# Leaving out two fills with zeros between the attention stage and the experts of a fused kernel

## The chip, the cores and the metric

One core of a Trainium2 chip runs one program. The metric is the device time of an execution in microseconds (us); less is better. The engines named below are TensorE (PE, with its weight loads as PEld), VectorE (DVE), ScalarE (ACT), GpSimd (POOL) and SyncE (SP), which issues most transfers.

## The reference, cut to what matters

```python
for t in range(S):                                   # attention: 2 x 8 heads, 768 steps, 48 wide
    state = alpha[:, :, t, :, None] * state + einsum('bhd,bhe->bhde', k[:, :, t], v[:, :, t])
    y[:, :, t] = einsum('bhd,bhde->bhe', q[:, :, t], state)
# x = y as 1536 tokens of 384 values
expert_idx = argmax(x @ w_gate, axis=1)              # one of 8 experts for each token, softmax weight gate_w
for i in range(N):                                   # at most `capacity` tokens for one expert
    if counts[e] < capacity: disp[e, counts[e]] = x[i]; pos[i] = counts[e]; counts[e] += 1
y = relu(disp[e] @ w1[e]) @ w2[e]                    # 384 -> 1024 -> 384
out[i] = gate_w[i] * y[expert_idx[i], pos[i]]
h = out @ w_in                                       # second block, 384 -> 2048 -> 384
return (h * clip(h + 3, 0, 6) / 6) @ w_out
```

## The kernel before, in words

The program has three stages, and the order of the work in each is written out by hand, engine by engine; every engine takes its instructions in that order, and an instruction that waits holds up those behind it on its engine.

**Attention and routing** (to about 122 us). The tokens are 12 tiles of 128. The work goes through 48 pairs (head pair, chunk of 128 tokens). After each tile its logits are turned into an expert and a place, and GpSimd scatters the tile's rows, multiplied by their gates, to a table `xdisp` in memory that has 256 rows for each of the 8 experts (`scatter`, line 119). For the first ten tiles this is done here. Tiles 10 and 11 are ready last, and for the first expert they take another way: `near` (lines 494 to 517) finds out on VectorE which of the tile's tokens go to expert 0 and builds from it a matrix `P` of 128 x 256 that has each token's gate at its place; `near_mm` (line 522) multiplies the tile with it; `near_rows` (line 530) adds the rows of the ten tiles before, which `read_x(0)` (line 226, on SP's queue) has read back from `xdisp` into `xr`. The steps of `near` for the last tile, tile 11, are these; `lgn` are its logits, `m` is their maximum, `g` is a result of TensorE in PSUM:

```python
501  nc.vector.tensor_reduce(out=lg, in_=x[:, t, :, 48:56]..., axis=AX.X, op=ALU.add)
502  nc.vector.tensor_reduce(out=m, in_=lg, axis=AX.X, op=ALU.max)
504  nc.vector.tensor_scalar(out=ls, in0=lg, scalar1=m, scalar2=None, op0=ALU.subtract)
505  nc.vector.tensor_tensor(out=o0[:, n:n + 1], in0=lg[:, 0:1], in1=m, op=ALU.is_ge)
507  nc.scalar.activation(out=ex, in_=ls, func=ACTF.Exp, accum_out=s)
512  nc.tensor.matmul(out=g[:, 0:1], lhsT=upto, rhs=o0[:, n:n + 1], start=False, stop=True)
513  nc.vector.tensor_scalar(out=s, in0=s, scalar1=1e-9, scalar2=None, op0=ALU.add)
514  nc.vector.reciprocal(out=rec, in_=s)
516  nc.vector.tensor_scalar(out=P, in0=place, scalar1=g[:, 0:1], scalar2=rec, ...)
```

The end of the stage on TensorE is, in this order: `near_mm` of tile 10 (line 522, six matmuls), the three small matmuls of tile 11 that give `g` (lines 509, 511, 512), `near_rows` (line 530, twelve matmuls), `near_mm` of tile 11 (line 522, six matmuls). As each third of the sum is ready, `split_x` makes of it the two parts `xhi` (line 236, ScalarE) and `xlo` (line 237, VectorE) that the experts' matmuls read.

**Experts** (to about 287 us). For each expert eight hidden tiles of 128: `l1` (line 761, nine matmuls for each tile, then `hh` on ScalarE and `hl` on VectorE, lines 766 and 767) and `l2` (line 782, nine matmuls). Weights come on SP's queue through three buffers (line 251) and are split in two parts on ScalarE (`whi`, line 262) and on VectorE or GpSimd (`wlo`, line 274). In between, `finish` (lines 184 to 219) sends the last two tiles to the other experts: GpSimd issues two scatters of `xc` (line 119), then the read of expert 1's rows (line 226), then twelve scatters of token numbers and their read (line 219). From expert 1 on the rows come from `xdisp` and are transposed on TensorE (line 747).

The outputs of an expert go to two arrays in SBUF, `xth` and `xtl`, of 128 partitions x 3 x 1792 values (1536 tokens and one slot of 256). Each expert writes 256 columns from its own offset on, which is read from `offi` at run time (lines 786 and 787), and what lies behind its tokens is written over by the next expert. At the start of the stage, ahead of the first `l1`, stand the fills that the change is about:

```python
799  for t in (xth, xtl):
800      nc.gpsimd.memset(t.bitcast(F32), 0.0)
```

The two arrays lie in memory that tiles of the attention stage used before.

**Second block** (to the end). 2 groups of 768 tokens by 16 hidden tiles: `m1` (line 863) reads columns 0 to 1535 of `xth` and `xtl`, `m2` (line 891) gives the rows that GpSimd scatters to the output.

Of the kernel before, what the change touches and what calls it, by code (L numbers as in the profile page):

```python
# [7 lines left out]
F32 = mybir.dt.float32  # L8
# [10 lines left out]
NP = 8          # head pairs (batch x 4)  # L19
SEQ = 768  # L20
C = 128         # chunk of tokens
NC = SEQ // C
NT = 12         # token tiles
# [3 lines left out]
FE = 8          # 128-wide hidden tiles of one expert  # L27
F2 = 16         # 128-wide hidden tiles of the second block
SLOT = 256      # rows held for one expert
NEAR_T = 10     # the tiles from here on reach the first expert on a way of their own  # L30
HW = 56         # value columns and gate columns of one head
RP = 112        # rows of a head pair: 48, 16 of padding, 48
HR = ((0, 64), (64, RP))    # rows of the two heads
GT = 768        # tokens in one group of the second block
PIECES = {0: ((0, 1), (1, 3), (3, 6)), 1: ((0, 2), (2, 6))}  # chunks that become ready together
TAIL = 3        # hidden tiles of the second block that are left to the end
OWN = 4096      # marks a token of the first expert: larger than any place


# Doubles come as pairs of words. A single has the sign, the top bit and the last 7 bits of the double's  # L40
# exponent, and the first 23 bits of its fraction. As a single, a double's upper word orders like the
# double itself: TINY and HUGE are the words of 2**-127 and of the last double below 2**128, times 2**16,
# which turns the second bit of the word's exponent into that of the result.
TINY = 2.0 ** -15 * 2.0 ** 16
HUGE = (1.875 - 2.0 ** -23) * 2.0 ** 16 * 2.0 ** 16


def to_single(nc, out, raw):
    """out[P, N] = the doubles of raw[P, N, 2] as singles, cut to 24 bits; below 2**-126 it gives 0 or less
    than 2**-126."""  # L50
    lo, hi = raw[:, :, 0], raw[:, :, 1]
    bits = out.bitcast(I32)
    nc.scalar.activation(out=out, in_=hi.bitcast(F32), func=ACTF.Abs, scale=65536.0)
    yield
    nc.vector.tensor_scalar(out=out, in0=out, scalar1=TINY, scalar2=HUGE, op0=ALU.max, op1=ALU.min)
    yield
    nc.vector.tensor_scalar(out=bits, in0=bits, scalar1=4, scalar2=1, op0=ALU.logical_shift_left,
                            op1=ALU.logical_shift_right)
    yield
    nc.vector.scalar_tensor_tensor(out=bits, in0=lo, scalar=29, in1=bits, op0=ALU.logical_shift_right,  # L60
                                   op1=ALU.bitwise_or)
    yield
    nc.vector.scalar_tensor_tensor(out=bits, in0=hi, scalar=-2147483648, in1=bits, op0=ALU.bitwise_and,  # L63
                                   op1=ALU.bitwise_or)
# [3 lines left out]
def tile_kernel(ctx: ExitStack, tc: tile.TileContext, qka, vtok, vT, wg64, wg, cap, consts,  # L68
# [38 lines left out]
    # of the last two tiles: values and logits  # L107
# [9 lines left out]
    def scatter(group, dst, idx, src, rows):  # L117
        # every row goes to a place of its own, so scatters need no order among themselves
        ins = nc.gpsimd.indirect_dma_start(  # L119
            out=dst, out_offset=bass.IndirectOffsetOnAxis(ap=idx, axis=0),  # L120
            in_=src, in_offset=None, bounds_check=rows - 1, oob_is_err=False)
        tc.declare_no_dep(ins.ins, group=group, reason="rows of scatters are disjoint")
        tc.add_to_no_dep_group(group, ins.ins)
        scattered.setdefault(group, []).append(ins.ins)
# [8 lines left out]
    def gating(pl, lg, o, po, cum, g, t0, n, res):  # L133
        """Of n tiles of logits: one-hot o of the expert, place po among its tokens, gate weight gt (0 past
        the capacity). The yields let other work in between."""
# [7 lines left out]
        # the first expert with the largest logit: its entry of idxrev is the largest  # L143
# [29 lines left out]
    def rows(pl, t0, n, res):  # L173
        # row of the dispatch: SLOT * expert + position, out of reach from position SLOT on
        po = pos[:, t0:t0 + n]
        rr = pl.tile([128, n], F32, tag=f"rr{n}", name="rr")
        nc.vector.scalar_tensor_tensor(out=rr, in0=po, scalar=float(SLOT), in1=res["r"][:, :, 0],
                                       op0=ALU.is_lt, op1=ALU.mult)
        di = pl.tile([128, n], I32, tag=f"di{n}", name="di", bufs=4)
        nc.vector.scalar_tensor_tensor(out=di, in0=rr, scalar=float(SLOT * NE), in1=po,  # L180
                                       op0=ALU.subtract, op1=ALU.add, reverse0=True)
        return di

    def finish(ps):
        """The last two tiles to the other experts, and where each expert's tokens go in the second block."""
# [36 lines left out]
    def read_x(e):  # L222
        t = xe_p[e % 2].tile([128, 2, DM], F32, tag="xr", name="xr")
        # SP's queue has weights behind; GpSimd's has the scatters before
        eng = nc.gpsimd if e == 1 else nc.sync
        ins = eng.dma_start(out=t, in_=xdisp[e * SLOT:(e + 1) * SLOT].rearrange("(c p) d -> p c d", p=128))
        if e < 3:
            after_scatters("disp", ins)
        xr[e] = t
# [49 lines left out]
    # ================= attention and routing =================  # L279
    with ExitStack() as actx:  # L280
# [34 lines left out]
        def load_piece(p, n):  # L315
            # a piece's columns of decays, keys and queries, and the first of the next
            c0, c1 = PIECES[p][n]
            lo, hi = c0 * C + (n > 0), min(c1 * C + 1, SEQ)
            for o in (2 * SEQ, 0, SEQ):
                nc.sync.dma_start(out=raw[p][:, o + lo:o + hi], in_=qka[p, :, o + lo:o + hi])  # L320
# [117 lines left out]
        def stage_b(p, c):  # L438
# [18 lines left out]
            # each head's scores meet the values of both; its own half is read  # L457
# [32 lines left out]
        # The first expert starts before the rows of the last two tiles come back from memory: products with  # L490
        # a matrix that holds each token's gate at its place put them among the rows of the tiles before.
# [44 lines left out]
        def warm_up(n):  # L536
            # TensorE runs at half its clock until it has been busy for a while
            g = ps_g.tile([128, 512], F32, tag="g", name="g")
            for _ in range(n):
                nc.tensor.matmul(out=g, lhsT=ones, rhs=warm, start=True, stop=True)  # L540
# [5 lines left out]
        with tc.manual_schedule():  # L546
# [56 lines left out]
            for i, (p, c) in enumerate(iters):  # L603
# [7 lines left out]
                if i == 12:  # L611
                    nc.gpsimd.tensor_scalar(out=upto, in0=ident, scalar1=float(OWN), scalar2=None, op0=ALU.mult)
                    nc.gpsimd.tensor_tensor(out=upto, in0=upto, in1=cst[:, 256:384], op=ALU.add)
                    # OWN + place; OWN - 1 past the capacity
                    nc.gpsimd.tensor_scalar(out=place, in0=iota1, scalar1=capf, scalar2=None, op0=ALU.is_le)
                    nc.gpsimd.tensor_tensor(out=place, in0=place, in1=iota1, op=ALU.mult)
                    nc.gpsimd.tensor_scalar(out=place, in0=place, scalar1=float(OWN - 1), scalar2=None, op0=ALU.add)
# [62 lines left out]
    # ================= experts =================  # L680
# [37 lines left out]
    def advance_f():  # L718
        # one step of the work on the second block's weights
# [11 lines left out]
    with ExitStack() as ectx:  # L731
# [59 lines left out]
        with tc.manual_schedule():  # L791
# [7 lines left out]
            for t in (xth, xtl):  # L799
                nc.gpsimd.memset(t.bitcast(F32), 0.0)  # L800
# [3 lines left out]
            for i in range(n):  # L804
# [21 lines left out]
                # GpSimd takes over where VectorE has more of the second block's weights to do  # L826
# [12 lines left out]
    # ================= second block, tokens in the order of the experts =================  # L839
    with ExitStack() as fctx:  # L840
# [60 lines left out]
        # ---- the steps above hold where no decay exceeds 1, chunks decay by no more than 1e-15 and  # L901
        # no expert has more than SLOT tokens; the flag says that one of these fails
# [7 lines left out]
        def check():  # L910
# [6 lines left out]
            # 1 where all is well  # L917
# [13 lines left out]
        with tc.manual_schedule():  # L931
            seq = [(g, f) for g in range(2) for f in range(F2)]
            m1(*seq[0])
            for i, (g, f) in enumerate(seq):
                if i + 1 < len(seq):
                    m1(*seq[i + 1])
                # the last ones tile by tile, so that the rows go out while others are at work
# [20 lines left out]
def general_path(tc, nc, gating, ident, cst, capf, b3, qka, vT, wg, wpack, fpack, out, before):  # L958
    """The same computation for any decays and any load of the experts, with no thought of speed."""
    vr = vT.rearrange("k p t -> (k p) t")  # L960
    GN = 512
    with ExitStack() as ctx:
# [8 lines left out]
        # attention: the state of each (key, value) column by a scan over all tokens  # L971
        with tc.tile_pool(name="g_a", bufs=1) as a_p, tc.tile_pool(name="g_aps", bufs=1, space=PSUM) as aps:
# [29 lines left out]
            # gating of all tokens at once  # L1002
# [55 lines left out]
        # experts: every token by every expert, weighted by its gate  # L1058
# [10 lines left out]
        # second block  # L1069
# [91 lines left out]
```

## Time and profile before

| what | us |
|---|---|
| three runs | 502.42, 504.25, 505.02 |
| their median | 504.25 |
| span of the profiled execution, first to last instruction | 501.6 |

The page of the profile gives the profiled execution's span and no other time for it; the fastest of the three runs is 0.8 us longer than that span, the median 2.65 us. Busy shares of the span: PE 92%, PEld 87%, DVE 66%, ACT 50%, POOL 36%. The mean granted TensorE clock is 0.948 of full speed. All times in the rows below are counted from the span's start; "idle before" in square brackets is how long the engine stood idle before an instruction and what ended that.

### The profile page before, as it was taken

Reading aid. Unit: us, or ns where it says so; the run is one execution under the profiler, and the core shown is the slowest. Engines: PE = TensorE matmul, PEld = TensorE weight load, DVE = VectorE, ACT = ScalarE, POOL = GpSimd, SP = SyncE. Lnnn points to the kernel's source line nnn. Section 1 sums busy time; section 2 is a strip of 40 time slices with the busy share of each in tenths; the row PEclk is TensorE's granted clock in tenths of the full one; section 3 lists DMA queues with packets and bytes.
Section 4 is the critical chain, followed back from the end, with each engine's and each line's share of the span. In section 5 each row is a group of like instructions: output and inputs, shape, how many; then the busy total and the mean of one; then the engine's idle time right before and its main releaser. Section 6 shows DMA issues by size and latency. Waiting matters only on the chain.

```text
span 501.6 us, 8487 instructions
## 1 busy us (share of the span) xinstructions
PE 460.5 (92%) x3148; PEld 438.6 (87%) x3148; DVE 332.7 (66%) x647; ACT 251.4 (50%) x573; POOL 181.6 (36%) x133
## 2 busy tenths in 40 slices
PE   7959969997796899999999999999899999999993
PEld 4758858887695899899999999888899999999993
DVE  6768998577673688888877669888833444444341
ACT  3536645775143677677677554544433433333341
POOL 3335965864457054555545501221200220000003
PEclk8987985899598999999999999999999999999998
DMA  7999892141057697677776102332100031100002
GB/s 194 273 231 294 228 327 65 47 144 64 0 139 148 170 303 246 199 251 265 268 255 219 65 29 98 125 117 75 54 1 0 34 118 57 55 1 0 3 1 101
DMA packets 27539, 66.03 MB, mean 132 GB/s; under 512 B 2896, under 2 KB 14448, under 8 KB 26816
## 3 DMA queue, kind: packets, MB, share of 16 engines
q1 hardware_dynamic: 25408, 60.26, 40.1%
q0 software_dynamic: 2080, 5.13, 2.9%
q8 instruction: 27, 0.44, 0.4%
q14 instruction: 24, 0.20, 0.1%
HBM read 57.51 MB, written 7.87 MB: 130 GB/s over the span
## 4 chain that ended last, share of the span: by engine, by line
PE 48%; issue 22%; DVE 16%; DMA 4%; ACT 4%; POOL 2%; SPq 1%; another core or an unknown queue 0%; POOLq 0%; ACTq 0%; DVEq 0%
PE o L782 13%; PE h L761 13%; PE h L863 5%; PE y L464 4%; PE o L891 4%; DVE gl L877 4%; PE s L423 3%; DMA qka<-in_qka_dram 3%; PE y L461 2%; DVE fc L60 2%; ACT gh L874 2%; POOL out_dram L119 2%; DVE A L358 2%; DVE fc L63 2%; PE u L447 1%
## 5 line engine op out<-in xcount | busy, mean ns | idle before, releaser
L877 DVE SCALAR_TENSOR_TENSOR gl<-t,gh 128x384 fp32r<-128x384 f32 x64 | 47.9, 748 | 36.2 <-ACT gh L874 35.3
L274 POOL TENSOR_TENSOR wlo<-wraw,whi 128x768 fp32r<-128x768 f32 x24 | 51.1, 2135 | 55.9 <-ACT whi L262 41.6
L262 ACT ACTIVATE whi<-wraw 128x768 fp32r<-128x768 f32 (+1 forms) x68 | 55.0, 808 | 25.7 <-PE o L782 24.0
L867 ACT ACTIVATE r<-h,b 128x384 f32<-128x384 f32 x64 | 36.6, 572 | 60.2 <-PE h L863 60.1
L871 DVE SCALAR_TENSOR_TENSOR t<-r,h 128x384 f32<-128x384 f32 x64 | 35.2, 550 | 46.6 <-ACT r L867 46.5
L891 PE MATMUL o<-fh,gl 128*128 128x384 f32 x192 | 64.1, 334 | 0.0
L891 PE MATMUL o<-fh,gh 128*128 128x384 f32 x192 | 64.1, 334 | 0.0
L891 PE MATMUL o<-fl,gh 128*128 128x384 f32 x192 | 64.1, 334 | 0.0
L119 POOL DMA_INDIRECT out_dram<-o,ids x12 | 12.0, 1000 | 124.1 <-DVE o L897 120.5
L782 PE MATMUL o<-hh,whi 128*128 128x256 f32 x192 | 54.5, 284 | 2.3 <-DVE xtl L787 1.4
L274 DVE TENSOR_TENSOR wlo<-wraw,whi 128x768 fp32r<-128x768 f32 (+1 forms) x41 | 42.9, 1047 | 19.7 <-ACT whi L262 17.6
L782 PE MATMUL o<-hl,whi 128*128 128x256 f32 x192 | 54.5, 284 | 1.2 <-DVE hl L767 1.0
L782 PE MATMUL o<-hh,wlo 128*128 128x256 f32 x192 | 53.9, 281 | 0.0
L712 POOL TENSOR_TENSOR fl<-fc,fh 128x768 fp32r<-128x768 f32 x16 | 31.0, 1938 | 63.1 <-ACT fh L710 63.1
L874 ACT ACTIVATE gh<-t 128x384 fp32r<-128x384 f32 x64 | 33.4, 523 | 39.9 <-DVE t L871 39.9
L863 PE MATMUL h<-xth,fh 128*128 128x384 f32 x192 | 45.0, 341 | 4.8 <-DVE t L871 4.7
L863 PE MATMUL h<-xtl,fh 128*128 128x384 f32 x192 | 43.7, 335 | 0.0
L863 PE MATMUL h<-xth,fl 128*128 128x384 f32 x192 | 43.6, 334 | 0.0
L402 ACT ACTIVATE kh<-qka,ra 64x128 f32<-64x128 f32 x96 | 38.1, 397 | 6.8 <-POOL qka L369 3.0
L863 PEld LDWEIGHTS h<-xth,fh 128*128 128x128 f32 x192 | 33.5, 188 | 7.7 <-DVE t L871 7.0
L761 PE MATMUL h<-xhi,whi 128*128 128x256 f32 x192 | 36.6, 296 | 3.8 <-issue 3.7
L782 PEld LDWEIGHTS o<-hh,whi 128*128 128x128 f32 x192 | 36.5, 190 | 3.0 <-DVE xtl L787 1.6
(168 smaller groups left out, 1099.4 us busy)
## 6 DMA issues: line engine op xcount, KB each, us to landing
wraw<-in_wpack_dram SPq DMA_DIRECT2D x32, 768.0 KB, 4.4
fr<-in_fpack_dram SPq DMA_DIRECT2D x16, 768.0 KB, 5.5
qka<-in_qka_dram SPq DMA_DIRECT2D x6, 1011.1 KB, 12.6
xdisp<-warm SPq DMA_DIRECT2D x1, 3072.0 KB
al<-in_qka_dram SPq DMA_DIRECT2D x8, 339.1 KB, 3.0
xr<-xdisp SPq DMA_DIRECT2D x7, 384.0 KB, 4.9
vx<-in_vtok_dram SPq DMA_DIRECT2D x6, 224.0 KB, 5.2
vx<-in_vtok_dram SPq DMA_DIRECT2D x2, 672.0 KB, 19.3
```

The lines of the kernel that those rows point to most:

```text
L262: nc.scalar.activation(out=w_sp[i][0][:, cols], in_=w_raw[i][:, cols], func=ACTF.Copy)
L274: eng.tensor_tensor(out=lo[:, cols], in0=w_raw[i][:, cols], in1=hi.bitcast(F32)[:, cols], op=ALU.subtract)
L402: nc.scalar.activation(out=t[r0:r1, h, :], in_=kb[p][r0:r1, c * C:(c + 1) * C], func=ACTF.Copy, scale=ra[p][r0:r1, c:c + 1])
L712: nc.gpsimd.tensor_tensor(out=lo, in0=t, in1=hi.bitcast(F32), op=ALU.subtract)
L761: nc.tensor.matmul(out=ps[:, 0:SLOT], lhsT=a[:, kk * 128:(kk + 1) * 128], rhs=b[:, kk, :], start=(n == 0), stop=(n == 8))
L782: nc.tensor.matmul(out=yo[e][d][:, 0:SLOT], lhsT=a[:, c0:c0 + 128], rhs=b, start=(f == 0 and n == 0), stop=(f == FE - 1 and n == 2))
L863: nc.tensor.matmul(out=ps[:, 0:384], lhsT=a[:, kk * 128:(kk + 1) * 128], rhs=b[:, kk, c0:c0 + 384], start=(n == 0), stop=(n == 8))
L867: nc.scalar.activation(out=r, in_=ps[:, 0:384], func=ACTF.Relu, bias=b3)
L871: nc.vector.scalar_tensor_tensor(out=t, in0=r, scalar=6.0, in1=ps[:, 0:384], op0=ALU.min, op1=ALU.mult)
L874: nc.scalar.activation(out=gh[:, sl], in_=t, func=ACTF.Copy, scale=1.0 / 6.0)
L877: nc.vector.scalar_tensor_tensor(out=gl[:, sl], in0=t, scalar=1.0 / 6.0, in1=gh.bitcast(F32)[:, sl], op0=ALU.mult, op1=ALU.subtract)
L891: nc.tensor.matmul(out=po[g][t][:, 0:DM], lhsT=a[:, t * 128:(t + 1) * 128], rhs=b[:, 384:768], start=(f == 0 and n == 0), stop=(f == F2 - ...
```

## The change: the fills of `xth` and `xtl` are not issued

```diff
@@ experts, ahead of the first l1
-            for t in (xth, xtl):
-                nc.gpsimd.memset(t.bitcast(F32), 0.0)
             step(3)
             l1(0)
```

Lines behind it move up by two (`values_load`, line 822, becomes line 820). Comments are taken out as well, without moving other lines.

On GpSimd, at the seam between attention and experts, the row of the order that the two programs have there (`xs` and `xc` are rows of tokens, `di` their places, `xdisp` the table in memory, `xr` the rows read back):

```order
 L485 TENSOR_SCALAR xs<-x,gt 128x384
 L119 DMA xdisp<-xs,di 2048x384 x5
-L800 MEMSET xth 128x5376
-L800 MEMSET xtl 128x5376
 L119 DMA xdisp<-xc,di 2048x384 x2
 L226 DMA xr<-xdisp 128x2x384
```

The two fills are gone and nothing else on GpSimd has changed its place; on the other engines the order of the instructions is the same as before. What changes beside that are waits. On GpSimd, the same place in the changed program with the semaphores that each instruction waits for:

```order
L119 DMA xdisp<-xs,di 2048x384 [waits DVE_49,Activation_49] x4
L119 DMA xdisp<-xc,di 2048x384 [waits DMAHW1_49,DVE_49,Activation_49]
L119 DMA xdisp<-xc,di 2048x384 [waits DMASW3_49,DVE_49,Activation_49]
L226 DMA xr<-xdisp 128x2x384 [waits DMASW4_49,DMASW3_49,DMASW5_49,DMASW2_49,DMASW6_49,DMASW1_49,DMASW7_49,DMASW0_49,PE_49]
L119 DMA idsd<-tokid,si 1536x1 [waits DVE_49]
```

The wait for TensorE (`PE_49`) stood at the first fill before; it now stands at the read of expert 1's rows, whose buffer lies in memory of the attention stage too. The first scatter of `xc` waits for ScalarE as well. The first writes of `xth` and `xtl` (lines 786 and 787) waited for GpSimd, and wait for it no longer.

## Rows read from the trace of the kernel before

**Rows 1.** Stretches: us, busy PE, PEld, DVE, ACT, POOL, granted clock, DMA share, GB/s.
```profile
121.50:126.20 4.70, 1.31 (x8) 0.99 (x8) 4.34 (x4) 0.36 (x3) 4.67 (x2) 0.94 0.00 2
...
180.00:230.00 50.00, 48.89 (x412) 48.43 (x411) 41.38 (x63) 35.74 (x68) 27.65 (x13) 1.00 0.75 254
```

**Rows 2.** Chain that ended last, 121 to 137 us: start us, us, what.
```profile
122.22 3.91 DVE ls L504
...
126.96 3.85 DVE P L516
```

**Rows 3.** Timeline of POOL: start us, us, engine, line, operation [idle before].
```profile
121.53 4.58 POOL L800 MEMSET xth<- 128x5376 f32 x1 [4.12 <-PE y L464]
126.05 4.60 POOL L800 MEMSET xtl<- 128x5376 f32 x1
```

**Rows 4.** Timeline of DVE, tile 10's steps, then tile 11's.
```profile
118.86 0.23 DVE L504 TENSOR_SCALAR ls<-lgn,m 128x8 f32<-128x8 f32 x1
119.00 0.15 DVE L505 TENSOR_TENSOR o<-lgn,m 128x1 bf16<-128x1 f32 x1
...
120.09 0.42 DVE L516 TENSOR_SCALAR P<-place,g,rec 128x256 f32<-128x256 f32 x1
...
122.03 0.16 DVE L502 TENSOR_REDUCE m<-lgn 128x1 f32<-128x8 f32 x1
...
126.50 0.15 DVE L513 TENSOR_SCALAR s<-s 128x1 f32<-128x1 f32 x1 [0.37 <-ACT ex L507]
```

**Rows 5.** Timeline of PE, 121 to 136 us.
```profile
121.30 1.04 PE L522 MATMUL s<-P,xc 128*128 128x256 f32 x4
122.18 0.59 PE L522 MATMUL kp<-P,xc 128*128 128x256 f32 x2
...
122.64 0.16 PE L511 MATMUL g<-o,ones 128*128 128x1 bf16 x1
126.21 0.16 PE L512 MATMUL g<-o,upto 128*128 128x1 bf16 x1 [3.41 <-DVE o L505]
126.24 2.06 PE L530 MATMUL s<-cst,xr 128*128 128x128 f32 x8
...
130.85 2.08 PE L522 MATMUL s<-P,xc 128*128 128x256 f32 x4 [1.70 <-DVE P L516]
...
135.90 0.52 PE L761 MATMUL h<-xhi,whi 128*128 128x256 f32 x3
```

**Rows 6.** Busy time by stretch, where the granted clock changes (columns as in rows 1).
```profile
125.50:126.00 0.50, 0.00 (x0) 0.00 (x0) 0.50 (x2) 0.00 (x0) 0.50 (x1) 0.62 0.00 0
...
127.00:131.00 4.00, 2.30 (x12) 2.00 (x10) 3.79 (x1) 0.00 (x0) 3.65 (x1) 0.50 0.00 0
...
135.80:136.20 0.40, 0.40 (x5) 0.40 (x5) 0.00 (x0) 0.00 (x0) 0.00 (x0) 0.92 0.00 0
```

**Rows 7.** Chain of the attention stage: four matmuls of 128 columns at full clock.
```profile
115.96 0.46 PE s L423 x4
```

**Rows 8.** Timelines of ACT and DVE: the last third of expert 0's rows is split.
```profile
133.81 0.39 ACT L236 ACTIVATE xhi<-kp 128x256 fp32r<-128x256 f32 x1 [0.47 <-PE kp L522]
...
134.23 0.42 DVE L237 TENSOR_TENSOR xlo<-kp,xhi 128x256 fp32r<-128x256 f32 x1 [0.43 <-ACT xhi L236]
```

**Rows 9.** SP's queue: the read of expert 0's rows, and its time to landing.
```profile
119.09 0.37 SPq L226 DMA_DIRECT2D xr<-xdisp  x1
...
DMA to landing us min/median/max: 3.0/3.0/3.0
```

**Rows 10.** VectorE's groups by form: the gates of the last two tiles.
```profile
L193 DVE TENSOR_SCALAR xc<-xc,gt 128x384 f32<-128x384 f32 x2 | 0.7, 414 | 0.0
```

**Rows 11.** Timeline of ACT: a later wait, in expert 0.
```profile
156.26 0.39 ACT L236 ACTIVATE xhi<-t 128x256 fp32r<-128x256 f32 x1 [3.27 <-remote]
```

**Rows 12.** Timelines of POOL and PE: expert 1's rows are read, then transposed.
```profile
144.28 0.78 POOL L226 DMA_DIRECT2D xr<-xdisp  x1 [2.31 <-issue]
...
149.52 0.38 PE L747 MATMUL t<-cst,xr 128*128 128x128 f32 x2
```

## The prediction

> **What bounds the kernel now.** I read the stages first. Through the experts TensorE is the bound: in the 50 us of [rows 1]'s second stretch it works 48.89 us at full clock. The stretch at 121.50, where the fills run, is another matter: TensorE works 1.31 us of 4.70, while VectorE and GpSimd look full, and the transfers move 2 GB/s. Then I read the chain of waits there. It does not go through GpSimd at all. It goes through two small VectorE instructions of the last tile, `ls` and `P`, with 3.91 and 3.85 us [rows 2]. The same two lines took 0.23 and 0.42 us one tile earlier [rows 4]. So something holds VectorE, and the timeline of GpSimd says what: the fill of `xth` runs from 121.53 to 126.11, the fill of `xtl` from 126.05 to 130.65 [rows 3]. `ls` starts at 122.22 and ends at 126.13, 0.02 us after the first fill; `P`, whose instruction record is 3.83 us long, ends at 130.79, 0.14 us after the second. Other VectorE instructions ran at their usual speed inside the fills: `m` took 0.16 us, `s` 0.15 us [rows 4]. I read this as two instructions of one kind (a tensor and a scalar per partition) that wait until GpSimd's fill has ended, and not as a VectorE that is slow as a whole.
>
> TensorE pays three times. It waits 3.41 us for `o`, the instruction right behind `ls`, and 1.70 us for `P` [rows 5]. And the granted clock: TensorE is idle from 122.80 on (122.64 + 0.16, [rows 5]), and in the stretch 125.50:126.00 the clock falls to a mean of 0.62; full speed is back only in 135.80:136.20 (0.92) [rows 6]. In between it runs at 1.2 GHz instead of 2.4.
>
> **The change, part by part.** *Removed:* two fills on GpSimd, 4.58 + 4.60 = 9.18 us of that engine [rows 3]. On GpSimd itself they cost nothing now: its next work stands behind the sums of `finish`, which come later than the fills. What counts is what they hold up. I follow the last tile without them.
>
> 1. `ls` starts at 122.22 as now, since `m` before it is not held. From its start to the end of `o` tile 10 needed 119.15 - 118.86 = 0.29 us [rows 4], so `o` is there at 122.51. TensorE is not ready for it before 122.67: line 511 starts at 122.64 and 512 can follow 0.03 later, as 530 follows 512 [rows 5]. So 512 starts at 122.67 instead of 126.21, and line 530 at 122.70 instead of 126.24: **3.54 us**.
> 2. Line 530 reads `xr`. Its transfer was issued at 119.09 and needs 3.0 us to land [rows 9], so it is there at 122.1, 0.6 us ahead. Nothing new is late here, but the cover is thin.
> 3. The twelve matmuls of line 530 take 130.85 - 1.70 - 126.24 = 2.91 us now, at half clock. With the gap gone TensorE works on without a stop, and I take the full clock: four fp32 matmuls of 128 columns take 0.46 us [rows 7], twelve 1.38. They end at 124.08: **1.53 us**.
> 4. `P`: in tile 10 it ended 120.51 - 118.86 = 1.65 us after `ls` began [rows 4], other work in between included. That gives 122.22 + 1.65 = 123.87, and with the 0.06 us from `P` to the matmul now (130.79 to 130.85) 123.93. TensorE is busy until 124.08, so the wait of **1.70 us** goes, by a margin of 0.15.
> 5. The six matmuls of line 522, the split and the first `l1` take 135.90 - 130.85 = 5.05 us now, up to the first matmul of the second `l1` [rows 5]. At full clock the six take 1.47 us until their results are there (121.30 to 122.18 + 0.59): 125.55. `xhi` of the last third starts 0.03 later and `xlo` 0.42 behind it, for 0.42 us [rows 8]: 126.42. Then four matmuls of 256 columns are left, at 0.12 us each (three `xhi` matmuls at 135.90 are followed after 0.36), and some 0.05 us for the semaphore: 126.95. So 2.87 instead of 5.05: **2.18 us**.
>
> The sum is 3.54 + 1.53 + 1.70 + 2.18 = **8.95 us**: 5.24 in waits, 3.71 from the clock. The two VectorE records alone would say 3.68 + 3.41 = 7.1 us; that is not the sum, because `P`'s delay lies partly beside line 530, and the clock is not in it.
>
> *Behind this point* I let everything move by the same 8.95 us. The order is the same on all engines, the weights' loads wait for buffers that TensorE's progress frees, hardly a byte moves in the first stretch of [rows 1], so no transfer sets a time of its own, and TensorE bounds the stages that follow. *Waits moved:* the wait for TensorE at the first fill ended at 121.53 [rows 3]; at the read of expert 1's rows it guards the same old memory, and I cost it at nothing, since that read is due at 144.28 - 8.95 = 135.33 [rows 12], 14 us later. The waits for GpSimd at the first writes of `xth` and `xtl` were over with the fills, long before these writes: nothing. The first scatter of `xc` also waits for ScalarE, which copied `xc` ahead of the matmuls of line 522 that read it: nothing.
>
> The profiled span of 501.6 us becomes 492.65. That execution's span is 2.65 us under the median of the three runs, and I carry that over: 504.25 - 8.95 = **495.3 us**.
>
> **The rivals.**
>
> *The clock stays low.* Only the waits go, 5.24 us, for **499.0 us**. For it: TensorE ran at 1.2 GHz (0.50) from there to 135.8, through 5 us of steady work at the end. Against it: the fall lies in 125.50:126.00 [rows 6], inside the gap that the change closes, and the longest new gap by my times is under 0.5 us, at the split.
>
> *`P` is held by something other than the fill.* Its record ends 0.14 us after the fill's, where `ls` ends at 0.02, and one of its scalars comes from PSUM. Alone it needs 0.42 us for 256 columns, while `xc`, of the same kind but with its operands in SBUF, needs 0.414 us for 384 [rows 10]; so `P` runs in a slower way than its kin, and may not need what the fill occupies. Then it starts at 122.22 + (120.09 - 118.86) = 123.45, still takes 3.83 us, and line 522 starts at 127.34 instead of 124.08. 3.26 us of the gain are lost: 8.95 - 3.26 = 5.69, or **498.6 us**. Against it: no other cause in the trace ends where `P` ends.
>
> The Trainium skill has a rule that speaks for this rival. Its page "SBUF — State Buffer", section "Who interferes with whom", says that VectorE and GpSimd share one pair of ports and that a VectorE instruction with one SBUF tensor needs that pair only in its two-port modes; "VectorE: DVE Perf Modes", section "Why PSUM operands drop a tier", says that a PSUM operand rules those modes out. If a scalar counts as an operand, that would free `P` from the fill and leave its 3.4 us in place. The row's coincidence in time outweighs it for me, hence a small chance only.
>
> *The gain is given back later.* ScalarE waits 3.27 us, until 156.26, for something the profile does not name [rows 11]. If what ends this wait does not depend on the chain, an earlier start only makes it longer, by up to all 8.95 us: between 495.3 and **504.25 us**. Against it: in every other wait from 137 to 166 us the releaser moves with the chain.
>
> *Slower: the moved wait.* The read of expert 1's rows now waits for TensorE on GpSimd's queue, with twelve scatters behind it. If that wait meant a TensorE instruction of the experts instead of one of the attention stage, the rows would be late for the transposes. The read is issued at 144.28 and used at 149.52 [rows 12]; with 3.0 us to landing 2.2 are to spare. It decides from 8.95 + 2.2 = 11.2 us of delay on: a wait of 15 us would give **508 us**. Against it: the same wait stood at the fill, and ended at 121.53.
>
> That the change does not do what it says is excluded by the order: both fills are gone, and no engine has got others.
>
> **How the numbers follow.** Forecast 0.76, clock stays low 0.10, `P` held otherwise 0.04, given back 0.08 (half of it leaving a gain above 2.5 us), slower 0.02. A measurement of this kernel can tell about 0.5%, 2.5 us, from no change. Faster by more than that: 0.76 + 0.10 + 0.04 + 0.04 = 0.94; within it: 0.04; slower: 0.02. The range runs from 493.0 (the fastest run before, 502.42, less a gain of 9.4) to 499.2, which takes in both partial gains, and leaves out the give-back and the slow case.
>
> **What would show it.** In the changed profile `ls` takes about 0.23 us and `P` about 0.42; line 512 starts near 122.7 with no wait, line 530 runs in about 1.4 us, the clock stays at 1.00 from 116 to 137 us, and the second `l1` starts near 127.0. From there to the end the distance is the same as now, 365.7 us (501.6 - 135.90). A clock of 0.50 in that stretch, a `P` of 3.8 us, a longer wait at `xhi` in expert 0, or a wait of POOL at line 226 would each name the step that failed.

## The result, and the profile after

Four executions of the changed kernel took 490.54 to 493.61 us, median 491.93, beside four of the kernel before with 502.42 to 505.02, median 503.85. The ratio is 0.9749, with a 95% interval of 0.9708 to 0.9791. The direction was forecast; the time, 495.3 us, was 3.4 us too high, and the measured median lies 1.1 us below the range. The comparisons, here and below, leave out the few executions that took over 1.5% more than the fastest of the same kernel in its set; with the six of the kernel before that fall to this, the mean difference given below as 8.74 us would be 9.4.

The page of the changed kernel, its span and part 1 (busy time of each engine):

```profile
span 491.8 us, 8482 instructions
...
PE 454.3 (92%) x3148; PEld 434.2 (88%) x3148; DVE 325.4 (66%) x647; ACT 251.3 (51%) x573; POOL 168.8 (34%) x131
```

The profiled execution's own time is 493.61 us, 1.81 more than its span. The seam (from here on: from the first matmul of line 522 to the first matmul of the second `l1`) ran as written down. VectorE's timeline, where rows 2 and 4 stood before:

```profile
119.10 0.23 DVE L504 TENSOR_SCALAR ls<-lgn,m 128x8 f32<-128x8 f32 x1
119.24 0.16 DVE L505 TENSOR_TENSOR o<-lgn,m 128x1 bf16<-128x1 f32 x1
...
120.16 0.42 DVE L516 TENSOR_SCALAR P<-place,g,rec 128x256 f32<-128x256 f32 x1
```

And TensorE's timeline, which answers to [rows 5]:

```profile
118.18 1.04 PE L522 MATMUL s<-P,xc 128*128 128x256 f32 x4
...
119.52 0.16 PE L511 MATMUL g<-o,ones 128*128 128x1 bf16 x1
119.54 0.16 PE L512 MATMUL g<-o,upto 128*128 128x1 bf16 x1
119.57 1.14 PE L530 MATMUL s<-cst,xr 128*128 128x128 f32 x8
...
120.99 1.03 PE L522 MATMUL s<-P,xc 128*128 128x256 f32 x4
...
123.96 0.52 PE L761 MATMUL h<-xhi,whi 128*128 128x256 f32 x3
```

`ls` and `P` have their usual 0.23 and 0.42 us, line 512 follows 511 without a wait, and both waits in square brackets of [rows 5] are gone. The seam is 123.96 - 118.18 = 5.78 us, where it was 135.90 - 121.30 = 14.60: 8.82 us less, beside 8.95 predicted. The stretch has the full clock (columns as in rows 1); the first row is the kernel before, the second the changed one:

```profile
121.30:135.90 14.60, 9.45 (x39) 8.00 (x37) 10.54 (x15) 2.00 (x8) 9.12 (x2) 0.65 0.01 3
```
```profile
118.18:123.96 5.78, 5.73 (x39) 4.88 (x37) 3.27 (x14) 2.00 (x8) 0.00 (x0) 1.00 0.00 0
```

But the spans differ by 9.8 us, and the medians by 11.9. The rest is not at the seam: it already began 3.1 us earlier (118.18 against 121.30), in a stage in which no instruction had changed. Later some of it is lost again. Two stretches of the changed kernel, and a row of its list of waits (engine, line, what it waited for: total us, times, longest):

```profile
151.00:159.00 8.00, 0.72 (x7) 0.54 (x7) 2.16 (x3) 1.85 (x3) 0.00 (x0) 0.69 1.14 130
159.00:164.20 5.20, 5.20 (x25) 5.20 (x26) 0.88 (x3) 1.68 (x4) 1.07 (x1) 0.50 0.87 263
```
```profile
PE t L747 <- DMA xr<-xdisp: 7.3, 1, 7.3
```

TensorE waits 7.3 us for the rows of expert 2, and comes back at 1.2 GHz (0.50 in the second stretch). Before there were other waits near this place, among them that of [rows 11]. So the question for the runs was: is the difference beyond 8.8 us the change's, or is it how these stages differ from one execution to the next?

### The profile page after: what moved, and what is told of

Its sections match the earlier page's. It is cut to its first block, busy times and chain, and to the rows that moved or that the text cites. A ratio compares the mean times of both kernels' runs of the same rounds, so it can differ in the third digit from the quotient of the medians.

```text
span 491.8 us, 8482 instructions
## 1 busy us (share of the span) xinstructions
PE 454.3 (92%) x3148; PEld 434.2 (88%) x3148; DVE 325.4 (66%) x647; ACT 251.3 (51%) x573; POOL 168.8 (34%) x131
## 4 chain that ended last, share of the span: by engine, by line
PE 67%; DVE 15%; DMA 8%; ACT 3%; issue 3%; SPq 1%; POOLq 0%; POOL 0%; ACTq 0%; DVEq 0%
PE h L861 15%; PE o L889 15%; PE o L782 12%; PE h L761 12%; DMA xr<-xdisp 4%; DVE gl L875 4%; PE y L464 3%; PE s L423 3%; DMA qka<-in_qka_dram 3%; PE y L461 3%; DVE fc L60 2%; ACT gh L872 2%; DVE fc L63 2%; DVE A L358 2%; PE u L447 1%
## 5 line engine op out<-in xcount | busy, mean ns | idle before, releaser
L782 PEld LDWEIGHTS o<-hl,whi 128*128 128x128 f32 x192 | 36.5, 190 | 1.6 <-DVE hl L767 1.6
L423 PE MATMUL s<-qka,kh 112*128 112x128 f32 x192 | 34.8, 310 | 3.1 <-DVE sc L426 2.3
## 6 DMA issues: line engine op xcount, KB each, us to landing
vx<-in_vtok_dram SPq DMA_DIRECT2D x2, 672.0 KB, 17.7
```

Of the source, the lines that this page charges most:

```text
L423: nc.tensor.matmul(out=s[:, h * C:(h + 1) * C], lhsT=kh[p, c][:, h, :], rhs=qh[p][:, lo:hi], start=True, stop=True)
L782: nc.tensor.matmul(out=yo[e][d][:, 0:SLOT], lhsT=a[:, c0:c0 + 128], rhs=b, start=(f == 0 and n == 0), stop=(f == FE - 1 and n == 2))
```

## The experiments

**The two kernels again.** No edit.

> The kernel before, unchanged, once more, for a second trace of it. Every theory expects no difference in time (ratio 1.00). The seam (first matmul of line 522 to the first matmul of the second l1) took 14.6 us before; the scatter theory (the seam's 9 us are all that the fills cost, and the rest of the measured difference is the spread from one execution to the next of the attention stage and of the stretch in which the token numbers are scattered) expects 14.6 again, while the attention stage and that stretch (second l1 to the first l1 of expert 3, 60.4 us before) come out differently by some us. The rival (the fills slow the attention stage or the experts too) expects attention near 121.3 and the stretch near 60.4 in every trace with the fills.

> The changed kernel once more: a ratio between 0.970 and 0.985. Scatter theory: the seam 5.7 us as in the first trace of it; the attention stage (118.2 us) and the stretch of the token numbers (62.2 us) each differ by 1 to 5 us from the first trace, in either direction. Rival (a lasting gain outside the seam): the attention stage near 118 again, 3 us under that of the kernel before.

> The changed kernel a third time, to see how far its median moves from chip to chip and from one set of runs to the next: seam 5.8 us; ratio between 0.975 and 0.985, median between 490 and 495 us. A ratio under 0.975 would speak for a gain beyond the seam.

The kernel before against itself: ratio 1.0006 (0.997 to 1.0042), with single executions from 498.7 to 505.3 us; the comparison's other executions of it go from 497.5 to 503.4. The changed kernel: 0.9841 (0.9789 to 0.9893) and 0.9834 (0.9778 to 0.989), medians 493.0 and 494.3. All the executions compared in these first two sets and the result's, 36 of the kernel before and 16 of the changed one, have means of 502.06 and 493.32 us: **8.74 us** apart, with a standard error of 0.6. Without the eight executions of the result itself it is 8.1 us, with a standard error of 0.7, so the 11.9 us between the result's medians did not come again. The traces say where they differ. The stretch is here from the second `l1` to the first `l1` of expert 3, the rest goes to the end:

| us | attention | seam | stretch | rest | span |
|---|---|---|---|---|---|
| before | 121.3 | 14.6 | 60.4 | 305.4 | 501.6 |
| before, again | 120.7 | 14.3 | 62.8 | 305.7 | 503.6 |
| changed | 118.2 | 5.8 | 62.2 | 305.7 | 491.8 |
| changed, again | 117.0 | 5.8 | 61.6 | 305.5 | 490.0 |
| changed, third | 119.1 | 5.8 | 61.2 | 305.2 | 491.3 |
| fills, numbers late | 119.0 | 14.5 | 52.3 | 305.5 | 491.3 |
| no fills, numbers late | 121.9 | 5.8 | 52.3 | 305.3 | 485.3 |
| the same, again | 117.2 | 5.8 | 52.3 | 305.5 | 480.8 |

In this table the seam goes with the fills and with nothing else. Attention does not: 119.0 to 121.3 with them, 117.0 to 121.9 without; in the traces of the runs below it goes down to 114.9 with both fills and to 116.6 without. What it goes with, roughly, is the granted clock. The whole stage in four traces (changed, again; before; no fills, numbers late; and the run with the clock kept, below), columns as in rows 1:

```profile
0.00:117.02 117.02, 99.04 (x772) 84.64 (x772) 93.93 (x241) 68.16 (x224) 67.28 (x66) 0.91 0.69 200
```
```profile
0.00:121.30 121.30, 104.98 (x771) 89.72 (x772) 94.03 (x241) 68.47 (x224) 67.48 (x66) 0.86 0.68 193
```
```profile
0.00:121.85 121.85, 110.70 (x771) 95.49 (x772) 91.98 (x241) 68.72 (x224) 61.50 (x66) 0.83 0.66 191
```
```profile
0.00:114.94 114.94, 95.87 (x772) 82.34 (x772) 94.31 (x241) 68.13 (x224) 65.73 (x66) 0.93 0.72 204
```

VectorE and ScalarE run the same instructions in all of them; the clock's mean is 0.93, 0.91, 0.86, 0.83 as the stage takes 114.9, 117.0, 121.3, 121.9 us. That is a relation and not a shown cause: no run here sets the clock of that stage by itself, and between the ends the order does not hold throughout (the kernel before, again, took 120.7 us at 0.89, the changed one 118.2 at 0.88).

**The token numbers late.** The twelve scatters of token numbers and their read are taken out of expert 0 and issued in the second block, once without and once with the fills:

```diff
         nc.vector.tensor_tensor(out=si, in0=sd[:, :, 0], in1=pos, op=ALU.add)
-        yield
+        sis.append(si)
+
+    sis = []
+
+    def place_ids():
         for t in range(NT):
-            scatter("ids", idsd[:, :], si[:, t:t + 1], tokid[:, t:t + 1], NT * 128)
+            scatter("ids", idsd[:, :], sis[0][:, t:t + 1], tokid[:, t:t + 1], NT * 128)
         after_scatters("ids", nc.gpsimd.dma_start(out=ids, ...))
...
+                if i == 9:
+                    place_ids()
```

> The changed kernel with the twelve scatters of token numbers and their read issued in the second block (after its tenth hidden tile) instead of in expert 0. If these scatters are what makes packets of weights take up to 6.9 us and leaves TensorE without rows and weights in experts 0 and 1, the stretch from the second l1 to expert 3 falls from 62.2 to about 52 to 54 us (22 hidden tiles at 2.13 us and 9 transposes, with no wait), the clock stays at full speed in it, and the time falls by 5 to 10 us below that of the changed kernel. If the slow packets have another cause (the weights' own loads, the reads of rows), the stretch stays at 60 us or more and the time within 2 us.

> The kernel before, fills in place, with the token numbers scattered in the second block in the same way. Scatter theory: against the run without the fills and with late numbers it is slower by the seam alone, 9.0 us (8 to 10), since what varied from execution to execution in experts 0 and 1 is gone from both. Rival (the fills cost some 12 us, in the seam and elsewhere): slower by 11 to 13 us.

> The changed kernel with late token numbers once more, on the same chip as the run above: seam 5.8 us, stretch from the second l1 to expert 3 52.3 us, median 484 to 488 us, ratio 0.960 to 0.972.

Without the fills: 0.9673 (0.9628 to 0.9717) of the kernel before, median 485.72 us, and in a later set 0.9701 (0.9634 to 0.9767), median 483.03. With the fills: 0.9817 (0.9765 to 0.9868), median 493.2. The 7.5 us between the two medians of the same set are a little below the 8 to 10 expected; in their traces attention alone differs by 2.8 us the other way. The stretch is 52.33 us in one and 52.36 in the other, without a stop, and the first row here is the seam with the fills:

```profile
119.01:133.53 14.52, 9.36 (x39) 7.89 (x38) 10.54 (x15) 2.00 (x8) 9.12 (x2) 0.65 0.02 6
133.53:185.86 52.33, 51.81 (x438) 51.26 (x437) 40.08 (x81) 34.14 (x64) 13.48 (x8) 1.00 0.64 216
```
```profile
127.64:180.00 52.36, 51.85 (x438) 51.30 (x437) 40.34 (x83) 34.19 (x64) 13.88 (x8) 1.00 0.65 216
```

With the scatters out of the way the experts run the same to 0.03 us, and the fills cost 14.52 - 5.79 = 8.73 us. What the scatters did is to be seen in the queues. The changed kernel, 140 to 148 us (queue: packets, MB, share of 16 engines; then issues with the median time to landing):

```profile
DMA packets 118, 0.22 MB, mean 27 GB/s; under 512 B 47, under 2 KB 47, under 8 KB 118
...
q1 hardware_dynamic: 74, 0.22, 74.9%
q0 software_dynamic: 44, 0.00, 0.4%
...
xr<-xdisp SPq DMA_DIRECT2D x1, 384.0 KB, 17.7
```

The same eight microseconds of the span with late numbers, where the second `l1` began 3.7 us later (a window moved by that much has 1.56 MB):

```profile
DMA packets 670, 1.76 MB, mean 220 GB/s; under 512 B 43, under 2 KB 155, under 8 KB 669
...
xr<-xdisp SPq DMA_DIRECT2D x1, 384.0 KB, 6.5
```

While packets of a few bytes are written, the weights' queue fills 75% of the engines' time and moves 0.22 MB; without them the core moves 1.76 MB in the same time. The rows of expert 2 land after 17.7 us instead of 6.5.

**One fill.** This run and the two behind it are one execution each (495.82, 495.70 and 496.10 us). Single executions of the kernel before went from 497.5 to 505.3 us, so only the stages are read from these runs, not the totals.

```diff
-            for t in (xth, xtl):
+            for t in (xth,):
                 nc.gpsimd.memset(t.bitcast(F32), 0.0)
```

> Only `xth` is filled; `xtl` is left as it is. By the sum of the prediction the wait for `ls` (3.5 us) and the low clock stay, and the wait of TensorE for `P` (1.7 us) goes: seam 14.6 - 1.7 = 12.9 us, `ls` 3.9 us, `P` 0.42 us. If the two delays on VectorE (3.7 and 3.4 us) were each paid in full, the seam would be 14.6 - 3.4 = 11.2 us. If half of all that the fills cost went with one fill: 10.2 us.

The seam took 10.99 us. VectorE's timeline, TensorE's, and the stretches of the seam from line 512 on (columns as in rows 1):

```profile
117.62 3.91 DVE L504 TENSOR_SCALAR ls<-lgn,m 128x8 f32<-128x8 f32 x1
...
122.37 0.42 DVE L516 TENSOR_SCALAR P<-place,g,rec 128x256 f32<-128x256 f32 x1
```
```profile
121.61 0.16 PE L512 MATMUL g<-o,upto 128*128 128x1 bf16 x1 [3.40 <-DVE o L505]
121.64 1.61 PE L530 MATMUL s<-cst,xr 128*128 128x128 f32 x8
...
123.89 1.85 PE L522 MATMUL s<-P,xc 128*128 128x256 f32 x4
```
```profile
121.60:123.90 2.30, 2.29 (x14) 2.29 (x13) 0.74 (x3) 0.27 (x2) 0.00 (x0) 0.62 0.00 0
123.90:127.69 3.79, 3.74 (x17) 2.92 (x17) 1.81 (x7) 1.37 (x4) 0.00 (x0) 0.78 0.00 0
```

`ls` is held as before and `P` is free, as expected; but the gain is 3.6 us and not 1.7, so this number was missed. The wait of 1.70 us went, and beyond it 1.9 us of clock: the engine, at work from 121.6 on without a second gap, has means of 0.62 and 0.78 where it had 0.50. So in this trace the wait cost about as much again in clock. That 11.2 us, expected if each of the two VectorE delays were paid in full, is near is chance: `P` was ready at 122.79 and TensorE at 123.89, so `P`'s delay had not been paid in full before.

**The clock kept.**

```diff
+            if n:
+                fill(20)
             nc.tensor.matmul(out=g[:, 0:1], lhsT=upto, ...)
...
             near_rows(acc)
+            fill(18)
```

> The kernel before with both fills; 20 matmuls of 384 columns on ones and zeros, whose result nobody reads, are put ahead of line 512's matmul for tile 11, and 18 behind line 530, so that TensorE is busy where it waited for `ls` and for `P`. The waits stay, the clock should not fall. By the prediction's terms the 2.18 us between line 522 and the second l1 are gained, and the 1.53 us of line 530 are hidden behind `P`: seam 14.6 - 2.2 = 12.4 us, clock 1.00 in it. If the low clock had cost nothing, or falls all the same: 14.6.

TensorE's timeline and the whole seam:

```profile
116.30 3.41 PE L546 MATMUL u<-warm,ones 128*128 128x384 bf16 x20
119.85 0.16 PE L514 MATMUL g<-o,upto 128*128 128x1 bf16 x1
...
121.29 3.09 PE L546 MATMUL u<-warm,ones 128*128 128x384 bf16 x18
```
```profile
114.94:127.56 12.62, 12.33 (x77) 8.59 (x75) 10.30 (x14) 1.99 (x8) 9.12 (x2) 1.00 0.01 2
```

The clock stays at 1.00 through waits of the same length, because TensorE has something to do in them, and the seam is 12.62 us: 1.98 less, 2.2 expected. The waits stay: the matmul of line 512 (514 here) starts 4.91 us after the seam began, as in the kernel before, and `near_mm` of tile 11 starts 4.64 us behind it, as before. What is left over the 5.78 us without the fills is theirs.

**Other forms of `ls` and `P`, with both fills in place.**

```diff
-            nc.vector.tensor_scalar(out=ls, in0=lg, scalar1=m, scalar2=None, op0=ALU.subtract)
+            nc.vector.tensor_tensor(out=ls, in0=lg, in1=m.to_broadcast([128, NE]), op=ALU.subtract)
...
-            nc.vector.tensor_scalar(out=P, in0=place, scalar1=g[:, 0:1], scalar2=rec, ...)
+            nc.vector.scalar_tensor_tensor(out=P, in0=place, scalar=g[:, 0:1],
+                                           in1=rec.to_broadcast([128, SLOT]), ...)
```

> The kernel before with both fills in place; only the forms of `ls` and `P` in lines 504 and 516 change, from one tensor with scalars to two tensors (a subtraction with the maximum spread over the columns, and a comparison with a product, whose second tensor is the reciprocal spread over 256 columns). If the fill holds exactly those VectorE instructions that work on one tensor and want a second way into memory, `ls` takes about 0.2 us and `P` about 0.45 with the fills running beside them, and the seam falls from 14.6 to about 5.8 us, as without the fills. Rival (a fill holds any VectorE instruction that starts a transfer of results while GpSimd writes, or semaphores are late): `ls` and `P` still take 3.8 us and the seam stays at 14.5.

GpSimd's timeline, VectorE's, and the whole seam:

```profile
117.99 4.58 POOL L801 MEMSET xth<- 128x5376 f32 x1 [4.34 <-PE y L464]
122.51 4.59 POOL L801 MEMSET xtl<- 128x5376 f32 x1
```
```profile
118.69 0.17 DVE L504 TENSOR_TENSOR ls<-lgn,m 128x8 f32<-128x8 f32 x1
...
119.68 0.49 DVE L516 SCALAR_TENSOR_TENSOR P<-place,g,rec 128x256 f32<-128x256 f32 x1
```
```profile
117.76:123.54 5.78, 5.74 (x38) 4.89 (x37) 3.28 (x14) 2.00 (x8) 5.55 (x2) 1.00 0.02 7
```

Both fills run, both operations run beside the first of them at 0.17 and 0.49 us, and the seam is 5.78 us as without the fills. So it is not the fill that costs, but a fill beside these two forms. `P` still takes a scalar from PSUM here and took one before, so that is not what decides. Behind the seam this one execution did worse: its stretch took 65.4 us, the longest of all, and expert 1's transposes waited for their rows, which they did in no other trace:

```profile
141.18 0.66 PE L748 MATMUL t<-cst,xr 128*128 128x128 f32 x2 [3.54 <-DMA xr<-xdisp]
```

Whether that comes of the kept fills or of the slow transfers beside the scatters is not shown.

**A form of the same kind beside GpSimd instructions that read.** On the version with late numbers, line 364 of the attention stage:

```diff
-                nc.vector.tensor_scalar(out=ra[p][:, c0:c1], in0=end, scalar1=1e-30, scalar2=None, op0=ALU.max)
+                nc.vector.scalar_tensor_tensor(out=ra[p][:, c0:c1], in0=end, scalar=1e-30, in1=end,
+                                               op0=ALU.max, op1=ALU.max)
```

> The changed kernel with late token numbers, and line 364 in the attention stage written with two tensors (the larger of the value, 1e-30 and the value again) instead of one tensor and a constant. In every trace six of these small operations (112x6) take 1.2 to 2.9 us instead of 0.14, and end where a multiplication on GpSimd (lines 369 and 372) ends. If the two-tensor form goes free beside any GpSimd instruction, as it did beside the fills, line 364 takes about 0.15 us each. If GpSimd instructions that read memory hold it in that form too, it still takes 1 to 3 us. The time should move by less than 2 us either way, since eight us of VectorE in that stage lie beside transfers and TensorE.

VectorE's groups by form, first with the old form (the run of late numbers, again), then with the new one:

```profile
L368 DVE TENSOR_SCALAR ra<-A 112x6 f32<-112x6 f32 x6 | 10.3, 1713 | 0.1
...
L368 DVE TENSOR_SCALAR ra<-A 112x4 f32<-112x4 f32 x1 | 0.1, 142 | 0.0
```
```profile
L368 DVE SCALAR_TENSOR_TENSOR ra<-A 112x6 f32<-112x6 f32 x6 | 10.0, 1669 | 0.1
```

Nothing is won: 1.67 us each instead of 1.71, while the same operation on 4 columns, where GpSimd is not multiplying, takes 0.14 in either form. With the new form the first of the six ends at 36.53 us, 0.02 after a multiplication on GpSimd that starts at 34.70 and takes 1.81. In these runs the two-tensor form goes free beside a fill, which only writes, and not beside GpSimd's multiplications, which also read. The time, 0.97 (0.9637 to 0.9762) of the kernel before, is that of the run beside it.

## Why the prediction was wrong, point by point

*Step 1, the wait for `ls`: right.* Line 512 starts 119.54 - 118.18 = 1.36 us after the first matmul of line 522; by the prediction 122.67 - 121.30 = 1.37.

*Steps 2 to 4: right.* The rows of `xr` were there. Line 530 took 120.99 - 119.57 = 1.42 us (1.38), and `P` ended at 120.58, 0.41 before it was needed. The margin was larger than the 0.15 estimated, because in tile 10 other work stood in between.

*Step 5: right.* 123.96 - 120.99 = 2.97 us (2.87). Sum of the seam: 8.82 us (8.95); over all traces with and without the fills 8.6 to 8.8.

*"Behind this point I let everything move by the same 8.95 us": right on the mean, and the place where the range failed.* The rest of the program is the same to 0.5 us in all traces. But attention before the seam and the stretch behind it are not fixed: 114.9 to 121.9 us over all traces, and 60.4 to 65.4 in those with the numbers at their old place, with the fills or without. The pair of profiles differs by 8.8 at the seam and 3.1 in attention, less 1.9 in the stretch and 0.3 in the rest: 9.8. The prediction looked at the seam as if everything else were constant.

*The base: wrong, and the step that failed.* "That execution's span is 2.65 us under the median of the three runs, and I carry that over" took one execution's distance from a median of three for something fixed. An execution takes 1.8 us more than its span (493.61 and 491.8); what is left of the 2.65 was spread. And the three runs happened to be slow: 504.25, where the 36 executions have a median of 502.44 and go from 497.5 to 505.3. So 1.8 us of the error are the starting point: 502.44 - 8.95 = 493.5 us, beside a median of 493.1 over the 16 executions of the changed kernel. Of the rest, 0.4 us lie between these two numbers, and 1.2 us, from 493.1 to the 491.93 of the four runs, are the same spread on the other side, which is luck. Executions and chips are not told apart here: in the last set, on another chip, the kernel before has a median of 500.3 us. The range was built from the three values ("the fastest run before, 502.42, less a gain of 9.4"), whose spread of 2.6 us says little of a spread of 8 between executions. The seam's term was sized right (8.82 for 8.95 us); it is this lower end of the range, 493.0 us, that the measured 491.93 broke.

*The rivals.* The clock did not stay low (1.00 in the seam). `P` was held by the fill and by nothing else; its two forms beside the fill settle that. The Trainium skill's page "VectorE: DVE Perf Modes" (section "Why PSUM operands drop a tier") keeps an instruction with a PSUM operand out of the two-port modes. That did not free `P` through its scalar in PSUM: `P` took 3.83 us beside the fill and 0.42 without. Whether the scalar makes `P` slower by itself (256 columns in 0.42 us, where `xc` does 384 in 0.414) stays open. The rule of the Trainium skill's page "SBUF — State Buffer" (section "Who interferes with whom"), that a VectorE instruction with two SBUF inputs contends with a GpSimd instruction that reads SBUF and not with one that only writes it, agrees with both runs on forms: 0.17 and 0.49 us beside fills, 1.67 us beside multiplications. *The gain is given back later* is not borne out: the stretch is 1.9 us longer in the changed kernel's first trace, but the two traces of the kernel before have 60.4 and 62.8 us, and the three of the changed one 61.2 to 62.2. That these 61 us could be 52 has to do with the token numbers and not with the change. *The moved wait* can be seen, and cost nothing. The read of expert 1's rows on GpSimd:

```profile
133.32 0.78 POOL L226 DMA_DIRECT2D xr<-xdisp  x1 [2.47 <-PE h L761]
```

The prediction named a wait of GpSimd at line 226 as a sign of this rival, and the row puts the wait down to an instruction of the experts, as do the other two traces of the changed kernel. But with the fills GpSimd stood idle there for 2.31 us as well [rows 12], so the read lost at most 0.16 us by it. It is issued 9.36 us after the second `l1` began, where it was 8.38, and the transposes of expert 1 did not wait for it.

## What to carry to other kernels

When a small vector instruction is many times longer than its twin elsewhere, look at what GpSimd runs at that moment: a fill that nobody waits for can hold it to its end, and the idle time costs again in TensorE's clock. Leaving the fill out and giving the held instruction two tensor operands are worth the same at this seam, and the second keeps the fill; that they are worth the same over the whole kernel is not shown. Before a range is built on three runs, find the stages whose length is not fixed (where the granted clock or the landing times vary), and give the base a spread of its own; compare stage by stage, since a seam measured to 0.1 us disappears in totals that move by 8.

## What the runs showed of the hardware

- The scatters of 1536 token numbers, some 6 KB in all, slowed the transfers beside them far beyond their bytes: 0.22 MB in 8 us where 1.76 MB went without them. Moving them to where few transfers run is worth another 7.3 us beside the change (medians of 485.7 and 493.0 us in one set), and no version here is clearly faster. What in the memory or the engines makes them so dear is not shown.
- Some VectorE operations with one tensor end where GpSimd's instruction ends: `ls` 0.02 us after the fill, in the kernel before and again with one fill (in the rows of that run 3.91 us long) and with the clock kept. Not all do: `m`, a reduction, took its usual 0.16 us inside the first fill, and `s`, a `tensor_scalar` too but on one column and with a constant, 0.15 us inside the second [rows 4]. No run here shows what makes the difference between `s` and `ls`. Whether the held ones wait at their start or at the write of their results is open.
